# Attention and greedy expert routing on one core: the first matrix product of the last two experts as seven block products

## The chip, the core and the metric

The kernel runs on one core of a Trainium2 chip. The metric is the device time of one execution in microseconds (us). The core has five engines with a queue each: PE (matrix multiply; its weight loads are shown as PEld), DVE (vector), ACT (activation), POOL (GpSimd) and SP, which here only starts DMA transfers and reads registers. An engine works through its queue in order; engines wait for each other through semaphores.

## The reference, cut to what matters

Clustered attention gives `x` (3072 tokens of 512). Each of 8 experts takes 384 tokens, chosen greedily by gate logits, and puts them through two matrix products with a ReLU between them:

```python
for e in range(E):                       # E = 8, cap = 3072 // 8 = 384 tokens each
    mask = assigned == e
    h = np.maximum(x[mask] @ w1[e], 0.0) # (384 x 512) @ (512 x 1024)
    out[mask] = h @ w2[e]                # (384 x 1024) @ (1024 x 512)
```

Inputs, weights and outputs are float32.

## The kernel before

The attention is the first part of the program and is not touched. In the second part the experts follow each other; in step names `p` is the place in this sequence (0 to 7), so "the last two experts" are p = 6 and p = 7. Which expert stands at a place, and which tokens it takes, is worked out on DVE with small PE products (steps `b`, `ind`, `cnt`, `c1` to `c3`, `gt`, `ge`, `rank`, `scan`, `col`, `pb0`, `pb1`, `rep`, `idx` and others), while the expert before is computed.

**Float32 as two float16.** Every operand is split into a high part, its value rounded to float16, and a low part, the rest. A product is three PE products: high by high, high by low, low by high.

**Work of one expert p.**
- `reg` reads the number of the expert into a register of SP; `w_load,p,c` loads eight 512 KB chunks of float32 weights into `wr0` to `wr7` (chunks 0 to 3: w1, 128 of the 512 input rows each; chunks 4 to 7: w2).
- `wsc` scales a chunk in place on ACT, `whi` writes its high part on ACT (`w1h`, `w2h`), `wlo` subtracts on POOL and writes its low part (`w1l`, `w2l`). These have two buffers each, by p % 2.
- `gx,p,g` fetches 128 tokens (indirect DMA, started by POOL), `xt` transposes them into `xgt` (started by SP). `xgt` holds high and low parts, 384 token columns each.
- `hid,p,f,c,i`: one PE product of 128x128 weights with 384 columns; f is one of 8 blocks of 128 hidden units, c one of 4 input chunks, i one of the three split products. 96 of these make the hidden layer of an expert. Their result lies in PSUM (`pf`, a pool of 5 banks).
- `rel,p,f` (ACT) writes the high part of ReLU, `hh`; `hlo,p,f` (DVE) the low part, `hl`.
- `out,p,g,f,i`: one PE product for 128 tokens g and hidden block f with 512 columns; 24 for each g, 72 for an expert. For p = 7, g = 2 it is cut in 384 and 128 columns (a fifth argument, 0 or 1).
- `oev` (ACT) scales the result into `ot`, `sc` (POOL) starts the indirect DMA that scatters it to the output.

**Order.** `FFN_ORDER` is one text of steps, executed one after the other when the program is built. Each step appends its instructions to its engine's queue, so the text fixes the order on every engine; the steps of different engines only wait for data and buffers. Before the change the text runs `hid` and `out` of p = 5, 6, 7 one after the other, with `rel`, `hlo`, `oev`, weight preparation and routing strewn in.

The routing state lies in PSUM (`pk`, one bank), so most DVE instructions of routing have a PSUM operand; `hlo` reads PSUM as well.

## Time and profile before

| what | value |
|---|---|
| time, median of 3 runs | 678.59 us (677.88 to 680.59) |
| time of the profiled execution | 678.19 us |
| span of its instructions | 676.4 us |
| mean granted TensorE clock | 0.969 |
| PE, DVE, ACT, POOL busy | 637.9, 498.5, 421.3, 512.9 us |

The span goes from the first to the last instruction; what lies between it and the execution's own time is 1.8 us. "Busy" adds up the recorded durations without their overlaps. A PE matmul is recorded from its issue to its modelled end, and the next is issued long before that, so the distance between two starts tells what a matmul costs, not its duration. A granted clock of 1 is 2.4 GHz, one of 0.5 is 1.2 GHz.

### The profile page before, as it was taken

Reading aid. Unit: us, or ns where it says so; the run is one execution under the profiler, and the core shown is the slowest. Engines: PE = TensorE matmul, PEld = TensorE weight load, DVE = VectorE, ACT = ScalarE, POOL = GpSimd, SP = SyncE. Lnnn points to the kernel's source line nnn. Section 1 sums busy time; section 2 is a strip of 40 time slices with the busy share of each in tenths; the row PEclk is TensorE's granted clock in tenths of the full one; section 3 lists DMA queues with packets and bytes.
Section 4 is the critical chain, followed back from the end, with each engine's and each line's share of the span. In section 5 each row is a group of like instructions: output and inputs, shape, how many; then the busy total and the mean of one; then the engine's idle time right before and its main releaser. Section 6 shows DMA issues by size and latency. Waiting matters only on the chain. (4 is left out here: it accounts for less than half of the span.)

```text
span 676.4 us, 19511 instructions
## 1 busy us (share of the span) xinstructions
PE 637.9 (94%) x8154; PEld 428.9 (63%) x8154; DVE 498.5 (74%) x1096; ACT 421.3 (62%) x560; POOL 512.9 (76%) x452
## 2 busy tenths in 40 slices
...
GB/s 239 140 144 199 210 156 214 144 149 206 207 115 177 196 143 100 167 73 74 29 51 72 25 234 108 267 105 286 182 209 226 179 222 168 240 302 206 47 1 47
DMA packets 175451, 105.85 MB, mean 156 GB/s; under 512 B 135426, under 2 KB 160002, under 8 KB 175362
## 3 DMA queue, kind: packets, MB, share of 16 engines
...
q8 instruction: 64, 1.05, 0.7%
q14 instruction: 25, 0.20, 0.1%
...
## 5 line engine op out<-in xcount | busy, mean ns | idle before, releaser
L842 POOL TENSOR_TENSOR rt<-pt 128x768 f16<-128x768 f32 x180 | 276.5, 1558 | 26.6 <-ACT pt L834 25.8
L834 ACT ACTIVATE pt<-sc 128x768 f32<-128x768 f32 x192 | 149.8, 811 | 93.9 <-PE sc L831 73.5
L792 DVE TENSOR_REDUCE mxs<-sc 128x1 f32<-128x768 f32 x192 | 176.1, 951 | 17.7 <-PE sc L788 17.2
L1457 PE MATMUL pf<-xgt,w1h 128*128 128x384 f16 (+1 forms) x640 | 130.2, 295 | 0.3 <-DVE xgt L752 0.2
L856 PE MATMUL av<-vh,rt 128*128 128x65 f16 x1152 | 120.6, 193 | 1.7 <-POOL rt L842 1.6
L853 PE MATMUL av<-vh,pt 128*128 128x65 f16 x1152 | 120.7, 194 | 1.1 <-DVE xb L889 1.1
L855 PE MATMUL av<-vl,pt 128*128 128x64 f16 x1152 | 120.4, 191 | 0.0
L855 PEld LDWEIGHTS <-pt 128*128 128x128 bf16 x1152 | 105.8, 98 | 8.6 <-issue 1.5
L853 PEld LDWEIGHTS <-pt 128*128 128x128 bf16 x1152 | 106.2, 97 | 7.3
L856 PEld LDWEIGHTS <-rt 128*128 128x128 f16 x1152 | 105.3, 97 | 1.9 <-POOL rt L842 1.9
L827 PE MATMUL sc<-qbt,kbt 99*128 99x384 f16 x384 | 94.4, 327 | 1.3 <-DVE mxs L792 0.7
L831 PE MATMUL sc<-qat,kat 128*128 128x384 f16 x384 | 94.4, 327 | 0.0
L788 PE MATMUL sc<-kbt,qbt 80*128 80x384 f16 x384 | 90.5, 330 | 2.2 <-DVE qbt L752 0.5
L1457 PE MATMUL pf<-xgt,w1l 128*128 128x384 f16 (+1 forms) x320 | 89.9, 295 | 0.0
L1415 ACT ACTIVATE wr<-wr 128x1024 f32<-128x1024 f32 x64 | 66.7, 1046 | 25.9 <-DMA wr<-in_moe_w_dram 25.3
L1457 PEld LDWEIGHTS <-w1h 128*128 128x128 f16 x640 | 58.0, 98 | 28.3 <-issue 0.9
L1499 PE MATMUL pf<-w2h,hh 128*128 128x512 f16 (+2 forms) x200 | 73.6, 370 | 0.0
L1499 PE MATMUL pf<-w2l,hh 128*128 128x512 f16 (+2 forms) x200 | 73.6, 370 | 0.0
L1499 PE MATMUL pf<-w2h,hl 128*128 128x512 f16 (+2 forms) x200 | 73.2, 370 | 0.0
L1425 POOL TENSOR_TENSOR w2l<-wr,w2h 128x1024 f16<-128x1024 f32 x32 | 67.6, 2133 | 7.3 <-ACT w2h L1418 6.8
L1425 POOL TENSOR_TENSOR w1l<-wr,w1h 128x1024 f16<-128x1024 f32 x32 | 67.4, 2133 | 1.5 <-ACT w1h L1418 1.3
L1489 DVE SCALAR_TENSOR_TENSOR hl<-pf,hh 128x384 f16<-128x384 f32 x56 | 30.9, 553 | 45.7 <-ACT hh L1486 40.2
...
## 6 DMA issues: line engine op xcount, KB each, us to landing
...
xg<-xrow,idx POOLq DMA_INDIRECT x24, 6.5
```

The source lines that it names most:

```text
L788: nc.tensor.matmul(p[:, half, :S // 2], QBT[u][:D + C, i, :], KBT[u][:D + C, h * J + half * 3:h * J + half * 3 + 3, :], start=True, stop=True)
L792: nc.vector.tensor_reduce(mxs[u % 3][:, i:i + 1], MP.pop((u, i))[:, :, :S // 2], axis=AX.XY, op=OP.max)
L827: nc.tensor.matmul(ps[:, half, :S // 2], KBT[u][:ER + 3, s, :], QBT[u][:ER + 3, cs, :], start=True, stop=False)
L831: nc.tensor.matmul(ps[:, half, :S // 2], KAT[u][:, s, :], QAT[u][:, cs, :], start=False, stop=True)
L834: nc.scalar.activation(pts[(u * 12 + s // 2) % RP][:, s % 2], MP.pop((u, "b", s))[:, :, :S // 2], AF.Exp, scale=ESC)
L842: (nc.vector if e == "D" else nc.gpsimd).tensor_sub(rts[x][:, s % 2], p.rearrange("p a b -> p (a b)"), hi_view(pts[x])[:, s % 2])
L853: nc.tensor.matmul(o[:, j, :D + 1], hi[:, js], VH[u][:, s, :D + 1], start=(kt == 0 and j == 0), stop=False, skip_group_check=True)
L855: nc.tensor.matmul(o[:, j, :D], hi[:, js], VL[u][:, s, :], start=False, stop=False, skip_group_check=True)
L856: nc.tensor.matmul(o[:, j, :D + 1], r[:, js], VH[u][:, s, :D + 1], start=False, stop=(kt == J - 1), skip_group_check=True)
L1425: nc.gpsimd.tensor_sub(lo, wrs[c], hi)
L1457: nc.tensor.matmul(o, (w1l if i == 2 else w1h)[x][:, c, fs], xgt[x][:, h + int(i == 1), ts], start=(first and i == 0), stop=(last and i == ...
L1499: nc.tensor.matmul(PS["o", p, g], (hl if i == 2 else hh)[x][:, f, g * P:(g + 1) * P], (w2l if i == 1 else w2h)[x][:, f, ds], start=(f == 0 ...
```

## The change

For p = 6 and p = 7 the 96 `hid` products, the `rel` and `hlo` steps, and `whi` and `wlo` of chunks 0 to 3 are gone. The product of w1 (transposed, 1024 x 512) with the tokens (512 x 384) is cut in 2 x 2 blocks: hidden halves by input halves for the weights (A11, A12, A21, A22), input halves by halves of 192 tokens. Seven block products replace eight, after the scheme of Strassen in Winograd's form:

- `sS,p,n,k` (DVE): the weight sums S1 = A22 + A21, S3 = A11 - A21, S2 = S1 - A11, S4 = A12 - S2, in float32, in place in `wr0` to `wr3`; k is one of two chunks, 512 columns each.
- `sh` (ACT) and `sl` (DVE or POOL, by its last letter D or P): high and low part of a block, 512 columns; A11, A12, A22 and the four sums, two chunks each, 14 of each step for an expert. The high parts lie in `sxh` or `w1h`, the low ones in `sxl` or `w1l`.
- `tx` (DVE): tokens high + low, float32, 1536 columns, into the `hh` buffer; `tt,p,n` (DVE): the token differences T1 to T4 (384 columns) into the `hl` buffer; `th` (ACT) and `tl` (DVE): their high and low part into `tsp`.
- `sp,p,n,q` (PE): block product n for half q of its hidden blocks: 12 matmuls of 192 columns; 14 such steps for an expert. M1, M6, M5, M3 add up in one bank `Z` for each q, M2 goes to `Y`, M7 and M4 to `X`.
- `cy` (ACT) copies `Z` between these additions to `zc`; `ad` (DVE) adds such a copy to `Y` or `X` into `sm`; `re` (ACT) and `hs` (DVE) write the high and low part of ReLU into `hh` and `hl`, eight of each (384 columns).

All steps of the text from `hid,5,2,0,1` on stand in another order: `hid,5` and `out,5` are mixed, the routing of p = 7 stands earlier or later, `out,6` and `out,7` run over all three g at once, `sc,5,1`, `sc,5,2` and `sc,6,2` stand much later. The steps themselves of p = 5, of the second products and of the routing are the same. In `f_out` and `f_oev` the key of the PSUM tile gets the part w of the columns, since both parts of p = 7, g = 2 are now open at the same time.

```diff
...
-oev,7,2,1 sc,7,2
...
+out,7,1,2,0 out,7,0,0,0 out,7,0,0,1 out,7,0,0,2 out,7,2,0,0,0 out,7,0,1,0 out,7,2,0,1,0 out,7,2,0,2,0 out,7,2,1,0,0
...
+    SH = F // 2
+    sxh, sxl = (ex.tile([P, 3, 2, SH], F16, name=n) for n in ("sxh", "sxl"))
+    tsp = ex.tile([P, 4, 2, 2, CAP // 2], F16, name="tsp")
+    zcs = [ex.tile([P, 2, CAP // 2], F32, name=f"zc{i}") for i in range(4)]
+    sms = [ex.tile([P, 2, CAP // 2], F32, name=f"sm{i}") for i in range(2)]
+    HOME = {"A11": 0, "A12": 1, "S2": 2, "S1": 0, "S3": 1, "S4": 2, "A22": 3}
+    RAW = {"A11": (0, 0), "A12": (0, 2), "A22": (1, 2), "S1": (1, 2), "S2": (0, 0), "S3": (1, 0), "S4": (0, 2)}
+    SUMS = {1: ((1, 2), (1, 0), (1, 2), OP.add), 3: ((1, 0), (0, 0), (1, 0), OP.subtract),
+            2: ((0, 0), (1, 2), (0, 0), OP.subtract), 4: ((0, 2), (0, 2), (0, 0), OP.subtract)}
+    half = (slice(0, CAP // 2), slice(CAP // 2, CAP))
+
+    def sraw(r, k):
+        return wrs[r[1] + k][:, r[0] * SH:(r[0] + 1) * SH]
+
+    def shome(p, b, k):
+        h = HOME[b]
+        if b in ("A11", "A12", "S2"):
+            return sxh[:, h, k, :], sxl[:, h, k, :]
+        c, o = 2 * (h // 2) + k, (h % 2) * SH
+        return w1h[p % 2][:, c, o:o + SH], w1l[p % 2][:, c, o:o + SH]
+
+    def f_sh(p, b, k):
+        nc.scalar.activation(shome(p, b, k)[0], sraw(RAW[b], k), AF.Copy)
+
+    def f_sl(p, b, k, e):
+        hi, lo = shome(p, b, k)
+        (V if e == "D" else nc.gpsimd).tensor_sub(lo, sraw(RAW[b], k), hi)
+
+    def f_sS(p, n, k):
+        o, a, b, op = SUMS[n]
+        V.tensor_tensor(sraw(o, k), sraw(a, k), sraw(b, k), op=op)
+
+    def sxf(p):
+        return hh[p % 2].rearrange("p f n -> p (f n)").bitcast(F32).rearrange("p (c n) -> p c n", c=DC)
+
+    def stt(p, n):
+        t = hl[p % 2].rearrange("p f n -> p (f n)").bitcast(F32).rearrange("p (t c n) -> p t c n", t=4, c=2)
+        return t[:, n - 1]
+
+    def f_tx(p):
+        x = xgt[p % 2].rearrange("p (c w) n -> p c w n", w=2)
+        V.tensor_tensor(sxf(p), x[:, :, 0, :], x[:, :, 1, :], op=OP.add)
+
+    def f_tt(p, n):
+        x = sxf(p)
+        b = lambda j, l: x[:, 2 * j:2 * j + 2, half[l]]
+        l, r = {1: (b(0, 1), b(0, 0)), 2: (b(1, 1), stt(p, 1)), 3: (b(1, 1), b(0, 1)), 4: (b(1, 0), stt(p, 2))}[n]
+        V.tensor_tensor(stt(p, n), l, r, op=OP.subtract)
+
+    def f_th(p, n):
+        nc.scalar.activation(tsp[:, n - 1, :, 0, :], stt(p, n), AF.Copy)
+
+    def f_tl(p, n):
+        V.tensor_tensor(tsp[:, n - 1, :, 1, :], stt(p, n), tsp[:, n - 1, :, 0, :], op=OP.subtract)
+
+    PROD = {1: ("A11", (0, 0)), 2: ("A12", (1, 0)), 3: ("S4", (1, 1)), 4: ("A22", 4), 5: ("S1", 1), 6: ("S2", 2), 7: ("S3", 3)}
+    ACC = {1: "Z", 6: "Z", 5: "Z", 3: "Z", 2: "Y", 7: "X", 4: "X"}
+
+    def f_sp(p, n, q):
+        blk, t = PROD[n]
+        z, first, last = ACC[n], n in (1, 2, 7), n in (3, 2, 4)
+        if first:
+            PS[z, q] = pff.tile([P, 2, CAP // 2], F32, name="pf")
+        for m in range(2):
+            fs = slice((2 * q + m) * P, (2 * q + m + 1) * P)
+            for k in range(2):
+                h, l = shome(p, blk, k)
+                if isinstance(t, int):
+                    xh, xl = tsp[:, t - 1, k, 0, :], tsp[:, t - 1, k, 1, :]
+                else:
+                    xh, xl = (xgt[p % 2][:, 2 * (2 * t[0] + k) + w, half[t[1]]] for w in range(2))
+                for i, (a, b) in enumerate(((h, xh), (h, xl), (l, xh))):
+                    nc.tensor.matmul(PS[z, q][:, m, :], a[:, fs], b, start=(first and m == 0 and k == 0 and i == 0),
+                                     stop=(last and m == 1 and k == 1 and i == 2), skip_group_check=True)
+
+    def f_cy(p, i, q, s):
+        nc.scalar.activation(zcs[s], PS["Z", q], AF.Copy)
+
+    def f_ad(p, z, q, s, o):
+        V.tensor_tensor(sms[o], PS[z, q], zcs[s], op=OP.add)
+
+    def sout(t, p, b, q):
+        i, l = b // 2, b % 2
+        f = 4 * i + 2 * q
+        return t[p % 2][:, f:f + 2, half[l]]
+
+    def f_re(p, b, q, o):
+        nc.scalar.activation(sout(hh, p, b, q), PS["Z", q] if o is None else sms[o], AF.Relu)
+
+    def f_hs(p, b, q, o):
+        V.scalar_tensor_tensor(sout(hl, p, b, q), PS["Z", q] if o is None else sms[o], 0.0, sout(hh, p, b, q),
+                               op0=OP.max, op1=OP.subtract)
+
...
     def f_out(p, g, f, i, w=2):
         ds = span(w)
         if f == 0 and i == 0:
-            PS["o", p, g] = pff.tile([P, ds.stop - ds.start], F32, name="pf")
+            PS["o", p, g, w] = pff.tile([P, ds.stop - ds.start], F32, name="pf")
         x = p % 2
-        nc.tensor.matmul(PS["o", p, g], (hl if i == 2 else hh)[x][:, f, g * P:(g + 1) * P], (w2l if i == 1 else w2h)[x][:, f, ds],
+        nc.tensor.matmul(PS["o", p, g, w], (hl if i == 2 else hh)[x][:, f, g * P:(g + 1) * P], (w2l if i == 1 else w2h)[x][:, f, ds],
                          start=(f == 0 and i == 0), stop=(f == FC - 1 and i == 2))
 
     def f_oev(p, g, w=2):
-        nc.scalar.activation(ots[(3 * p + g) % 4][:, span(w)], PS["o", p, g], AF.Copy, scale=1.0 / (SX * SW * SW))
+        nc.scalar.activation(ots[(3 * p + g) % 4][:, span(w)], PS["o", p, g, w], AF.Copy, scale=1.0 / (SX * SW * SW))
```

**PE, first product of p = 6.** What stood on PE before, in `hid` of p = 6 (`w1h_8026` and `w1l_8028` are the buffers of p = 6, `pf` the PSUM bank, `xgt_8038` the tokens):

```order
L1457 LDWEIGHTS w1h_8026
L1457 MATMUL pf<-xgt_8038,w1h_8026 128x384
L1457 LDWEIGHTS w1l_8028
L1457 MATMUL pf<-xgt_8038,w1l_8028 128x384
L1457 LDWEIGHTS w1h_8026
L1457 MATMUL pf<-xgt_8038,w1h_8026 128x384
```

and what stands there now, in `sp,6,2,1` (`sxh`, `sxl` hold the parts of A12):

```order
L1543 LDWEIGHTS sxh
L1543 MATMUL pf<-xgt_8038,sxh 128x192
L1543 LDWEIGHTS sxh
L1543 MATMUL pf<-xgt_8038,sxh 128x192
L1543 LDWEIGHTS sxl
L1543 MATMUL pf<-xgt_8038,sxl 128x192
```

Each matmul has half the columns, and there are 168 where 96 were; every one has its own weight load, as before.

**DVE, behind the routing of p = 7.** Before, from `ohv,7` (L1342) on; L1369 to L1382 are `pb0`, `pb1`, `pi`, `idx`, L1489 is `hlo`:

```order
L1342 TENSOR_TENSOR ohv<-ohl,pk 128x384
L1369 TENSOR_TENSOR cq_8009<-pc,own_189 128x192
L1372 TENSOR_REDUCE cs_8010<-cq_8009 128x24
L1379 SCALAR_TENSOR_TENSOR pg<-pc,own_189 128x24
L1382 TENSOR_REDUCE idx_8017<-pg 128x3
L1489 SCALAR_TENSOR_TENSOR hl_8042<-pf,hh_8040 128x384 x8
L1489 SCALAR_TENSOR_TENSOR hl_8043<-pf,hh_8041 128x384 x8
```

Now, behind `pb1,7`, during the block products of p = 6 (L1512 `tx`, L1518 `tt`, L1497 `sl`, L1501 `sS`, L1524 `tl`, L1370 and L1373 `pi`, `idx`, L1550 `ad`; `hh_8040` and `hl_8042` hold sums of tokens here, `tsp` the parts of T1 to T4):

```order
L1512 TENSOR_TENSOR hh_8040<-xgt_8038 128x1536
L1518 TENSOR_TENSOR hl_8042<-hh_8040 128x384 x2
L1497 TENSOR_TENSOR sxl<-wr_8018,sxh 128x512
L1518 TENSOR_TENSOR hl_8042<-hh_8040,hl_8042 128x384
L1501 TENSOR_TENSOR wr_8021<-wr_8021,wr_8019 128x512
L1524 TENSOR_TENSOR tsp<-hl_8042,tsp 128x2x192 x2
L1370 SCALAR_TENSOR_TENSOR pg<-pc,own_189 128x24
L1373 TENSOR_REDUCE idx_8017<-pg 128x3
L1550 TENSOR_TENSOR sm_8057<-pf,zc_8053 128x384
L1550 TENSOR_TENSOR sm_8058<-pf,zc_8054 128x384
L1524 TENSOR_TENSOR tsp<-hl_8042,tsp 128x2x192
L1497 TENSOR_TENSOR w1l_8028<-wr_8020,w1h_8026 128x512
```

Where two `idx` instructions and then the `hlo` of the expert stood, there are now 14 instructions: `tx` stands behind `pb1,7`, and everything that T1 to T4 need stands behind `tx` in the same queue; most of these instructions read two operands that both lie in SBUF.

**POOL, the last rows.** Before (L1425 `wlo`, L1506 `sc`; `w2l1` the low parts of w2 of p = 7, `ot2`, `ot3` and so on the results that are scattered):

```order
L1425 TENSOR_TENSOR w1l1_8029<-wr3_8021,w1h1_8027 128x1024
L1425 TENSOR_TENSOR w2l1_8033<-wr4_8022,w2h1_8031 128x1024
L1425 TENSOR_TENSOR w2l1_8033<-wr5_8023,w2h1_8031 128x1024
L1425 TENSOR_TENSOR w2l1_8033<-wr6_8024,w2h1_8031 128x1024
L1506 DMA out_0_dram<-ot2_8048,idx2_8016 3072x512
L1425 TENSOR_TENSOR w2l1_8033<-wr7_8025,w2h1_8031 128x1024
L1506 DMA out_0_dram<-ot3_8049,idx2_8016 3072x512
L1506 DMA out_0_dram<-ot0_8046,idx2_8016 3072x512
```

and now (L1497 `sl`, L1416 `wlo`, L1590 `sc`; `w1l1` the low parts of sums of p = 7):

```order
L1497 TENSOR_TENSOR w1l1_8029<-wr1_8019,w1h1_8027 128x512
L1497 TENSOR_TENSOR w1l1_8029<-wr3_8021,w1h1_8027 128x512 x2
L1416 TENSOR_TENSOR w2l1_8033<-wr4_8022,w2h1_8031 128x1024
L1590 DMA out_0_dram<-ot3_8049,idx2_8016 3072x512
L1416 TENSOR_TENSOR w2l1_8033<-wr5_8023,w2h1_8031 128x1024
L1416 TENSOR_TENSOR w2l1_8033<-wr6_8024,w2h1_8031 128x1024
L1416 TENSOR_TENSOR w2l1_8033<-wr7_8025,w2h1_8031 128x1024
L1590 DMA out_0_dram<-ot0_8046,idx2_8016 3072x512
L1590 DMA out_0_dram<-ot1_8047,idx3_8017 3072x512
L1590 DMA out_0_dram<-ot2_8048,idx3_8017 3072x512
```

The scatter `sc,6,1` (from `ot3`) stands between the first and the second w2 subtraction of p = 7, and the other three stand behind it.

## Rows read from the trace of the kernel before

**Rows 1.** The page's first part: busy time, share of the span, instructions.

```profile
PE 637.9 (94%) x8154; PEld 428.9 (63%) x8154; DVE 498.5 (74%) x1096; ACT 421.3 (62%) x560; POOL 512.9 (76%) x452
```

**Rows 2.** Windows from `hid,5,2` on: length, busy (instructions) by engine, clock, DMA, GB/s.

```profile
579.40:600.00 20.60, 20.60 (x122) 11.12 (x120) 15.31 (x51) 15.59 (x21) 11.77 (x8) 1.00 0.94 289
600.00:620.00 20.00, 20.00 (x116) 11.08 (x115) 4.00 (x9) 17.72 (x23) 16.57 (x12) 1.00 0.93 295
620.00:640.00 20.00, 20.00 (x102) 9.67 (x101) 1.67 (x3) 7.87 (x11) 16.25 (x10) 1.00 0.15 53
640.00:660.00 20.00, 20.00 (x116) 11.25 (x115) 4.46 (x8) 4.25 (x9) 0.74 (x1) 1.00 0.04 14
```

**Rows 3.** PE timeline: start, duration, line, form, count; widths 384, 128, 192.

```profile
611.78 0.33 PE L1457 MATMUL pf<-xgt,w1l 128*128 128x384 f16 x1
...
622.99 0.33 PE L1457 MATMUL pf<-xgt,w1l 128*128 128x384 f16 x1
...
668.55 0.22 PE L1499 MATMUL pf<-w2h,hh 128*128 128x128 f16 x1
...
669.84 0.22 PE L1499 MATMUL pf<-w2h,hl 128*128 128x128 f16 x1
...
585.05 0.42 PE L1365 MATMUL pc<-ohh,ohv 128*128 128x192 f16 x3
585.31 0.33 PE L1457 MATMUL pf<-xgt,w1h 128*128 128x384 f16 x1
```

**Rows 4.** The page's groups: weight loads of the first product.

```profile
L1457 PEld LDWEIGHTS <-w1h 128*128 128x128 f16 x640 | 58.0, 98 | 28.3 <-issue 0.9
```

**Rows 5.** Groups by form: line, operation, form, count | busy us, mean ns.

```profile
L877 DVE TENSOR_TENSOR av<-av,rc 128x384 f32<-128x384 f32 x31 | 17.6, 566 | 1.0
L1478 DVE SCALAR_TENSOR_TENSOR hl<-pf,hh 128x512 f16<-128x512 f32 x6 | 4.1, 685 | 0.1
L657 DVE SCALAR_TENSOR_TENSOR qa<-ld,qa 128x1536 f16<-128x1536 f32 x6 | 10.5, 1755 | 0.6 <-ACT qa L652 0.5
L1415 ACT ACTIVATE wr<-wr 128x1024 f32<-128x1024 f32 x64 | 66.7, 1046 | 25.9 <-DMA wr<-in_moe_w_dram 25.3 <-issue 0.6
L652 ACT ACTIVATE qa<-ld 128x384 f16<-128x384 f32 x4 | 2.1, 523 | 0.1
L1425 POOL TENSOR_TENSOR w2l<-wr,w2h 128x1024 f16<-128x1024 f32 x32 | 67.6, 2133 | 7.3 <-ACT w2h L1418 6.8
L659 POOL TENSOR_TENSOR qa<-ld,qa 128x384 f16<-128x384 f32 x4 | 3.6, 912 | 0.5 <-ACT qa L652 0.4
```

**Rows 6.** Timelines of POOL and DVE, attention: subtractions with both operands in SBUF.

```profile
339.84 2.89 POOL L842 TENSOR_TENSOR rt<-pt 128x768 f16<-128x768 f32 x2
...
343.06 5.74 POOL L842 TENSOR_TENSOR rt<-pt 128x768 f16<-128x768 f32 x3
...
343.39 4.09 DVE L842 TENSOR_TENSOR rt<-pt 128x768 f16<-128x768 f32 x2 [1.07 <-ACT pt L834]
...
359.86 3.68 DVE L842 TENSOR_TENSOR rt<-pt 128x768 f16<-128x768 f32 x4
```

**Rows 7.** PE and DVE timelines around the routing of p = 6.

```profile
586.12 0.33 PE L1457 MATMUL pf<-xgt,w1h 128*128 128x384 f16 x1
586.44 0.17 PE L1376 MATMUL pc<-cs,rep 128*128 128x24 f16 x1
...
579.53 0.40 DVE L1290 SCALAR_TENSOR_TENSOR mk<-pk,pc,mq 128x24 bf16<-128x24 f32 x2
...
585.91 0.48 DVE L1372 TENSOR_REDUCE cs<-cq 128x24 f16<-128x192 f16 x1
```

**Rows 8.** Timelines of POOL and SP: token fetches and transposes of p = 6.

```profile
587.43 0.98 POOL L1429 DMA_INDIRECT xg<-xrow,idx  x1 [9.29 <-DVE idx L1382]
...
594.98 5.36 SPq L1433 DMA_TRANSPOSE xgt<-xg  x3
```

**Rows 9.** Window at the switch from attention to experts, columns as in Rows 2.

```profile
375.00:380.00 5.00, 1.25 (x36) 1.11 (x32) 4.13 (x21) 0.00 (x0) 0.00 (x0) 0.56 0.15 43
```

More of the change, by code (lines that the diff above doesn't have):

```diff
@@ L368 @@
-hid,5,3,3,2 hid,5,4,0,0 ohl,6 w_load,6,5 hid,5,4,0,1 rel,5,3 hid,5,4,0,2 hid,5,4,1,0 ohh,6 hid,5,4,1,1 w_load,6,6
-hid,5,4,1,2 hid,5,4,2,0 hid,5,4,2,1 ohv,6 w_load,6,7 hid,5,4,2,2 hid,5,4,3,0 lt,6 col,6 wsc,6,0 upd,6 hid,5,4,3,1
-hid,5,4,3,2 pb0,6 hid,5,5,0,0 hid,5,5,0,1 hid,5,5,0,2 pb1,6 hid,5,5,1,0 rel,5,4 hlo,5,3 rep,6 hid,5,5,1,1 hid,5,5,1,2
-whi,6,0,C hid,5,5,2,0 pi,6 hid,5,5,2,1 hid,5,5,2,2 idx,6 hid,5,5,3,0 hlo,5,4 gx,6,0 hid,5,5,3,1 hid,5,5,3,2
-hid,5,6,0,0 wsc,6,1 b,7,0 hid,5,6,0,1 hid,5,6,0,2 hid,5,6,1,0 b,7,1 hid,5,6,1,1 hid,5,6,1,2 gx,6,1 b,7,2 hid,5,6,2,0
```

122 lines of the change are left out of this document (59 added, 63 removed).

## The prediction, on record before the changed kernel was run

> **What bounds the kernel now.** I read the page's first part first: PE is busy for 94% of the span, the next engines for 76% and 74% [rows 1]. That is a mean over unlike stages, so next came windows over the changed part, from `hid,5,2,0,1` at 579.4 us (call it T) on. There PE is busy all of the time at a granted clock of 1.00, while DVE has 15.3, 4.0, 1.7 and 4.5 us of work in stretches of 20, and POOL's load ends by 640 [rows 2]. The reader is to see that only PE sets the time here, and that the others have room, DVE most. Then I measured starts on the PE timeline, because a duration of a matmul overlaps the next: 69 matmuls of 384 columns take 622.99 - 611.78 = 11.21 us, 0.1625 each; 23 of 128 columns take 1.29, 0.0561 each [rows 3]. A line through both is 0.416 ns a column, which gives 0.0827 for 192 and 0.216 for 512. The only 192-column products are three of `col`; with the step to the next instruction they take 0.26, 0.087 each at most [rows 3]. Last I looked at waits: at `rep,6` PE stands 0.16 us beyond a matmul's 0.1625, behind the reduction `pb1,6` on DVE [rows 7]. From T the matmuls need about 90.5 us, to 669.84 + 0.22 = 670.06 [rows 3]. Behind them comes the last result and scatter, which the change leaves alone.
>
> **What it takes away and adds on PE.** An expert loses 96 x 0.1625 = 15.6 us and gets 14 x 12 = 168 matmuls of 192 columns, 168 x 0.0827 = 13.9. That is 1.7 less, for two experts **-3.4 us**. With 0.087 it is 168 x 0.087 = 14.6, together -2.0; with columns alone (7/8 of 15.6) it is -3.9. I take -3.4, since 384 and 128 columns lie on one line and 192 lies between. Weight loads number 168 where 96 stood. One is recorded with 98 ns [rows 4], yet matmuls of 128 columns, each with its own load, go by every 56 ns, so loads are hidden at a shorter distance than 83 ns.
>
> On that the Trainium skill disagrees ("TensorE: Matmul & The Clock Gate", section "Back-to-back issue gap"): it gives about 81 ns for each matmul of 128 columns and 131 for 512 in a stream with a load for each. On a straight line between them, an estimate, 192 columns would cost 89 ns and 384 some 114, and the two experts would lose 8 us. The trace has 56 and 162 ns for 128 and 384 columns, so I go by the rows.
>
> **What it adds elsewhere, hidden or not.** For both experts together DVE gets about 60 instructions more. By the nearest rows (0.57 for 384 columns, 0.69 for 512, 1.76 for 1536 [rows 5]) its work from T rises from 27 to 66 us, ACT's (0.52 for 384, some 0.63 for 512, 1.05 for 1024 [rows 5]) from 50 to 70; POOL keeps 48 (2.13 for 1024, 0.91 for 384, so 1.1 to 1.2 for 512 [rows 5]). All are below the 86.6 us that PE has to do from T on (90.0 before by counts, less 3.4), so the sums cost nothing; if anything costs, it is the order at single places. I put PE's steps in their new order with the prices above and walked the other queues against them; times are us behind T.
>
> 1. `rep,6`. PE gets there at 6.9. `pb1,6` ended at 7.0 before (585.91 + 0.48 less T) [rows 7]; now `hlo,5,1` and more routing stand ahead, I reckon 7.3. PE waits 0.5 where it waited 0.2: **+0.3**. If the walk is off, 0 to 1.
>
> 2. Block products of p = 6. `col,7` is on PE at 23.9 (71 `hid`, 53 `out`, 1 `sp` to `sp,6,2,1` and the routing's few). `pb1` ends 1.4 behind it, as it did for p = 6 (585.05 to 586.39 [rows 3, 7]), so at 25.3. Behind it on DVE stand `tx` 1.76, three `tt` 1.7, `sl` 0.69, `sS` 0.69, two `tl` 1.13, `pi` and `idx` 0.35 (an estimate from 0.20 for 24 columns [rows 7]), two `ad` 1.13, `tl` 0.57 and `sl,6,S1,0` 0.69: 8.7, ending at 34.0. PE needs the last of them for `sp,6,5,1`, at 34.7 by content (71 `hid`, 72 `out`, 7 `sp`), 35.2 with the wait above. So there is 1.2 us of room. Two things use it up. `tx` also needs the third token transpose: `gx,6,2` starts at about 13.8 on POOL, fetch to transpose takes 7.6 and a transpose occupies the queue for 1.8, three take 5.36 [rows 8], and SP issues weight loads beside it; it lands between 24 and 26, which is **+0.3** at most likely, 0 to 0.8. And `tx`, `tt`, `tl`, `sl`, `sS` read two SBUF operands, as POOL's subtractions do. Two such on DVE and POOL took turns in the attention: POOL alone took 1.45 each, overlapped 1.91; DVE alone 0.92, overlapped 2.04, so 1.1 more for each that meets one [rows 6]. POOL has `sl,6,S1,1` and `sl,6,S3,1` in this stretch, and perhaps `wlo,6,4`; two meetings are 2.2, beyond the room by 1.0. I take half of it, **+0.5**, with 0 and 5 as bounds (5: all of POOL's 2.13 + 2 x 1.2, and the fetches late too).
>
> The Trainium skill has this as a rule ("SBUF — State Buffer", section "Who interferes with whom"): a DVE instruction with two SBUF inputs and a GpSimd one share an exclusive lock, and the second waits in full. The trace agrees, with 0.92 against 2.04. By the rule in full it is the rival B below.
>
> 3. w2 of p = 7. POOL has `wlo,7,4`, `sc,6,1`, `wlo,7,5` to `wlo,7,7` at its end. `sc,6,1` waits for `oev,6,1`, which ACT ends at about 71.3, behind `whi,7,6`. A scatter's issue taken like a fetch's 0.98 [rows 8] and two `wlo` of 2.13 [rows 5] end at 76.6; with one meeting with DVE's `hs` on the way `wlo,7,6` is done at 77.0. A chunk of w2 serves two hidden blocks, so chunk 6 is first read by `out,7,0,4,1`: at 76.4 by content, a few tenths later with the waits so far. I take **+0.4**, 0 to 1.5. `wlo,7,7` at 79.2 to 79.7 then stands against `out,7,0,6,1` at 79.9.
>
> 4. Banks, given back by ACT and DVE between block products, and `tl,7,4`: **+0.2**, 0 to 1. Elsewhere the walk leaves 1 to 3 us.
>
> Together +1.7. The change is -3.4 + 1.7 = -1.7: the profiled 678.19 becomes 676.5. The median of the runs stands 0.4 above the profiled time, so I say **676.9 us**. For the clock I count nothing: it stood at 0.56 where PE was busy for 1.25 of 5 us [rows 9], and waits of tenths between full stretches are far from that.
>
> **Rivals.**
> - A, everything is on time: no wait beyond before's 0.2. 678.6 - 3.4 = 675.2. For it: sums of work on DVE and ACT are far below PE's. Against it: at places 1 and 3 the queues arrive at the same time as PE.
> - C, the gain is used up: places 2 and 3 near their upper bounds by turns, waits of 2.5 to 5.5 in all, 677.7 to 680.7. For it: two chains with 1 us of room each, worked out by hand.
> - B, slower: in the block products of p = 6 DVE loses its turns to POOL. Ten two-operand instructions stand between `pb1,7` and `sp,6,5,1`; if seven meet a POOL subtraction, 7 x 1.1 = 7.7, less the room of 1.2, is 6.5, and the same in the products of p = 7, where DVE is loaded as much, some 2 more, with 0.9 from places 1 and 3: waits of 8 to 9.5 and 678.6 - 3.4 + 8 = 683 or more. It decides when all waits exceed 3.4, and makes it slower by more than 0.5% from 6.8 on. Against it: POOL has only two to four subtractions in those 9 us, so at most four can meet.
> - D, weight loads bind: 168 x 0.098 = 16.5 against 15.6, +0.9 for each expert, 678.6 + 1.7 + 1.7 = 682.0. Against it stand the 56 ns of 128 columns [rows 3, 4].
>
> **How the numbers follow.** The forecast (675.5 to 678) has 0.60, A 0.16, C 0.13, B 0.09, D 0.02. The range of 675.0 to 680.0 holds the forecast, A's upper part and most of C, and leaves out B, D and the ends. Half a per cent, about what a measurement here can tell from no change, is 3.4 us: faster than 675.2 needs all of A and a bit of the pure column price, 0.11; slower than 682.0 is B and half of D, 0.09; the rest is 0.80. So it most likely gains a quarter of a per cent.
>
> **What would show it.** Starts of the 192-column products lie 0.083 apart (0.098 would be D). Gaps on PE stand at `rep,6`, ahead of S1 T1 in p = 6 (behind DVE), and at `out,7,0,4,1` (behind POOL), each under 1 us, and the granted clock stays at 1.00 to the end. POOL's `sl` and `wlo` and DVE's `tx`, `tl`, `sS` would last longer where they overlap; if DVE's are over 1.5 us in a row, it is B. If `tx,6` waits for a transpose and not for `pb1`, place 2 fails in its cause. A matmul end that moved by less than the sum of waits would make the columns' price wrong.

## The result, and the profile after

The changed kernel takes 688.27 us (median of 5 runs, 686.46 to 691.56) where the kernel before took 678.87 in the same comparison: a ratio of 1.0149, 95% interval 1.0118 to 1.0181. It is 9.4 us slower; 676.9 had been forecast. The profiled execution took 691.56 us, the longest of the five, with a span of 689.8 against 676.4. Of these 13.4 us, 2.8 stand ahead of everything that the change touches: the matmuls of the two traces drift apart at 15 to 25 us, in the attention, and the distance is still 2.77 where `hid,5,2,0,1` starts, at 582.17 (T) here and at 579.40 before. What follows counts from T. From T to the end of the span the changed kernel takes 107.6 us, the kernel before 97.0.

The page's first part after the change; it answers to [rows 1]:

```profile
PE 641.3 (93%) x8298; PEld 442.1 (64%) x8298; DVE 550.3 (80%) x1156; ACT 436.3 (63%) x600; POOL 516.3 (75%) x458
```

DVE has 51.8 us more than before. Waiting inside two of its instructions accounts for 10.3 of them, as will be seen. Windows of the changed kernel from T on, with the columns of [rows 2]:

```profile
582.17:622.40 40.23, 39.92 (x303) 26.54 (x300) 33.39 (x79) 31.27 (x51) 26.27 (x20) 1.00 0.70 229
622.40:627.00 4.60, 0.37 (x5) 0.14 (x3) 4.50 (x4) 0.16 (x1) 3.99 (x3) 0.86 0.94 246
627.00:632.50 5.50, 5.50 (x29) 4.22 (x28) 3.43 (x7) 5.47 (x10) 0.99 (x1) 0.50 1.12 268
632.50:666.70 34.20, 33.76 (x263) 22.91 (x262) 32.58 (x42) 23.25 (x41) 13.71 (x9) 1.00 0.09 33
666.70:670.00 3.30, 1.08 (x5) 0.31 (x4) 3.30 (x2) 0.00 (x0) 3.13 (x3) 1.00 0.00 0
670.00:673.50 3.50, 3.50 (x11) 1.34 (x10) 0.09 (x1) 0.00 (x0) 0.48 (x1) 0.52 0.20 75
673.50:681.80 8.30, 8.28 (x59) 4.68 (x56) 0.00 (x0) 1.57 (x3) 1.94 (x2) 1.00 0.09 34
681.80:689.80 8.00, 0.00 (x0) 0.00 (x0) 0.00 (x0) 0.30 (x2) 0.97 (x1) 0.62 0.17 66
```

The reader is to see two holes and what lies behind each. From 622.40 PE does almost nothing for 4.6 us while DVE and POOL are busy; then its granted clock is 0.50 for 5.5 us. From 666.70 the same again, shorter, with 0.52 for 3.5 us behind it. PE's rows at both holes and at `rep,6` (the last number in brackets is the idle time and who ended it):

```profile
589.02 0.33 PE L1448 MATMUL pf<-xgt,w1h 128*128 128x384 f16 x1
589.65 0.17 PE L1367 MATMUL pc<-cs,rep 128*128 128x24 f16 x1 [0.31 <-DVE cs L1363]
...
622.39 0.25 PE L1543 MATMUL pf<-xgt,w1l 128*128 128x192 f16 x1
626.86 0.50 PE L1543 MATMUL pf<-tsp,w1h 128*128 128x192 f16 x2 [4.23 <-DVE sm L1550]
...
667.17 0.38 PE L1583 MATMUL pf<-w2l,hh 128*128 128x512 f16 x1
669.67 0.39 PE L1583 MATMUL pf<-w2h,hl 128*128 128x512 f16 x1 [2.12 <-DVE hl L1561]
```

Start to start, less the product's own 0.08 or 0.216, the holes are 4.40 us (`sp,6,4`, A22 by T4) and 2.29 us (`out,7,0,4,2`, the first that reads `hs,7,2,0`). What DVE and POOL did there:

```profile
620.64 5.04 DVE L1524 TENSOR_TENSOR tsp<-hl,tsp 128x384 f16<-128x384 f32 x1 [0.24 <-ACT tsp L1521]
...
663.27 6.82 DVE L1561 SCALAR_TENSOR_TENSOR hl<-sm,hh 128x384 f16<-128x384 f32 x2
```

```profile
620.06 0.96 POOL L1420 DMA_INDIRECT xg<-xrow,idx  x1 [0.16 <-issue]
621.05 4.21 POOL L1416 TENSOR_TENSOR w2l<-wr,w2h 128x1024 f16<-128x1024 f32 x2
...
661.64 1.24 POOL L1590 DMA_INDIRECT out_dram<-ot,idx  x1 [3.34 <-ACT ot L1587]
662.91 6.28 POOL L1416 TENSOR_TENSOR w2l<-wr,w2h 128x1024 f16<-128x1024 f32 x3
```

`tl,6,4` takes 0.55 us elsewhere and 5.04 here: it ends 0.4 us behind the second of two w2 subtractions on POOL (621.05 + 4.21 = 625.26). The `hs` of p = 7, 0.55 elsewhere, stands at 663.27 and ends 0.4 us behind the third of three (669.19). `ad,6,X,0,0,0`, which the first hole names as releaser, is only the next but one behind `tl,6,4` in DVE's queue.

The sum, from T to the last matmul 99.61 us (to 681.78), where 90.66 had been needed, so 8.95 more (the first three terms give 9.0):

| term | us |
|---|---|
| 336 products of 192 columns at 0.0825 for 192 of 384 at 0.1625 | -3.5 |
| waits of PE: `rep,6` 0.47; `sp,6,4` 4.40; `sp,7,4` 0.39 + 0.38; `out,7,0,4,1` 0.26; `out,7,0,4,2` 2.29; less 0.22 before (0.16 of it at `rep,6`) | +8.0 |
| half clock behind the two long waits: 2.8 and 1.7, added up start to start against the prices at 1.00 | +4.5 |
| last matmul to the end of the span: 8.00 for 6.36 | +1.6 |
| together | +10.6 |

The last term was no part of the forecast either. POOL's scatters and ACT's results at the end of the changed kernel:

```profile
676.22 0.97 POOL L1590 DMA_INDIRECT out_dram<-ot,idx  x1 [5.74 <-ACT ot L1587]
680.53 0.97 POOL L1590 DMA_INDIRECT out_dram<-ot,idx  x1 [3.34 <-issue]
684.01 0.97 POOL L1590 DMA_INDIRECT out_dram<-ot,idx  x1 [2.51 <-issue]
```

```profile
675.35 0.60 ACT L1587 ACTIVATE ot<-pf 128x512 f32<-128x512 f32 x1 [11.70 <-PE pf L1583]
677.72 0.60 ACT L1587 ACTIVATE ot<-pf 128x512 f32<-128x512 f32 x1 [1.78 <-PE pf L1583]
681.42 0.68 ACT L1587 ACTIVATE ot<-pf 128x384 f32<-128x384 f32 x2 [3.10 <-PE pf L1583]
```

The first result is ready at 675.95 and its scatter starts 0.27 us later. The other two are ready at 678.3 and 682.1, yet their scatters start at 680.53 and 684.01, about 2 us later. In the kernel before the last scatter started 0.27 us after its result (670.38 and 670.65).

### The profile page after: what moved, and what is told of

Its sections match the earlier page's. It is cut to its first block, busy times and chain, and to the rows that moved or that the text cites. A ratio compares the mean times of both kernels' runs of the same rounds, so it can differ in the third digit from the quotient of the medians.

```text
span 689.8 us, 19884 instructions
## 1 busy us (share of the span) xinstructions
PE 641.3 (93%) x8298; PEld 442.1 (64%) x8298; DVE 550.3 (80%) x1156; ACT 436.3 (63%) x600; POOL 516.3 (75%) x458
## 5 line engine op out<-in xcount | busy, mean ns | idle before, releaser
L1448 PE MATMUL pf<-xgt,w1h 128*128 128x384 f16 (+1 forms) x512 | 99.5, 288 | 0.3 <-DVE xgt L743 0.2
L1416 POOL TENSOR_TENSOR w2l<-wr,w2h 128x1024 f16<-128x1024 f32 x32 | 67.9, 2145 | 8.5 <-ACT w2h L1409 8.1
L1448 PE MATMUL pf<-xgt,w1l 128*128 128x384 f16 (+1 forms) x256 | 69.3, 288 | 0.0
L1583 PEld LDWEIGHTS <-hh 128*128 128x128 f16 x400 | 37.8, 99 | 34.9 <-issue 2.4
L1448 PEld LDWEIGHTS <-w1h 128*128 128x128 f16 x512 | 45.7, 99 | 20.1 <-issue 0.7
L1590 POOL DMA_INDIRECT out_dram<-ot,idx x24 | 24.7, 1030 | 42.7 <-ACT ot L1587 33.6
```

Of the source, the lines that this page charges most:

```text
L1416: nc.gpsimd.tensor_sub(lo, wrs[c], hi)
L1448: nc.tensor.matmul(o, (w1l if i == 2 else w1h)[x][:, c, fs], xgt[x][:, h + int(i == 1), ts], start=(first and i == 0), stop=(last and i == ...
L1583: nc.tensor.matmul(PS["o", p, g, w], (hl if i == 2 else hh)[x][:, f, g * P:(g + 1) * P], (w2l if i == 1 else w2h)[x][:, f, ds], start=(f = ...
```

## The experiments

Each kernel was timed beside the kernel before. The last column is the time from T to the end of the span in the profiled execution (97.0 in the kernel before). T itself lies between 577.97 (a1) and 582.97 (c3) in these profiles, though the attention is the same in all, so the medians of a few executions carry scatter that the last column leaves out; it comes from one execution each. Where the intervals of two ratios overlap, as those of a1, a2 and a3 do with the changed kernel's, the times alone don't tell them apart, and the argument rests on the traces.

| kernel | median us | before us | ratio (95%) | T to end, us |
|---|---|---|---|---|
| changed kernel | 688.27 | 678.87 | 1.0149 (1.0118 to 1.0181) | 107.6 |
| a1_whi_late | 684.79 | 677.68 | 1.0119 (1.0100 to 1.0138) | 102.7 |
| a2_w2l_dve | 684.54 | 677.68 | 1.0110 (1.0090 to 1.0130) | 103.4 |
| a3_fill | 684.35 | 677.68 | 1.0118 (1.0087 to 1.0150) | 104.2 |
| a4_wlo_first | 687.26 | 677.68 | 1.0156 (1.0139 to 1.0173) | 104.2 |
| c1_dve_all | 684.68 | 679.32 | 1.0082 (1.0057 to 1.0106) | 102.2 |
| c2_dve_tail | 682.65 | 679.32 | 1.0060 (1.0026 to 1.0094) | 101.2 |
| c3_whi76_late | 691.02 | 679.32 | 1.0171 (1.0144 to 1.0197) | 109.6 |
| c4_order | 686.80 | 679.32 | 1.0106 (1.0068 to 1.0144) | 105.9 |
| d1_late_tail | 681.11 | 678.37 | 1.0036 (1.0015 to 1.0057) | 99.4 |
| d2_whi76 | 686.72 | 678.37 | 1.0126 (1.0088 to 1.0164) | 104.8 |
| d3_no_pool | 680.97 | 678.37 | 1.0040 (1.0025 to 1.0055) | 99.3 |
| d4_no_sl | 677.99 | 678.37 | 0.9995 (0.9978 to 1.0012) | 97.1 |
| e1_oev_early | 680.99 | 679.39 | 1.0024 (1.0011 to 1.0036) | 97.8 |
| e3_hs_early | 680.95 | 678.52 | 1.0034 (1.0015 to 1.0052) | 97.8 |

**The wait at `sp,6,4`.** In a1_whi_late POOL's first w2 subtraction is held back until `tl,6,4` can have its turn:

```diff
 re,6,0,1,1 cy,6,b,0,2
-whi,6,7,C
 wlo,6,5,C
...
 th,6,4
+whi,6,7,C
 tl,6,4
```

> One step is moved on ACT: whi,6,7 stands behind th,6,4, so POOL's wlo,6,7 cannot start before th,6,4 is done, and DVE's tl,6,4 (5.04 us in the changed kernel, beside two wlo of POOL from 621.05 to 625.25) gets its turn ahead of them. Theory 1 (POOL's run of subtractions keeps DVE's two-SBUF instruction out, and the clock falls to 0.50 because PE stood still): tl,6,4 takes under 1 us, PE's wait of 4.40 us ahead of sp,6,4 shrinks under 1 us, and the stretch at half clock behind it (2.9 us lost) is gone too; with the p = 7 part as it was, the median goes from 688.3 to about 681 (680 to 683). Theory 2 (tl,6,4 is late because T4 itself or its high part comes late): the wait stays above 3 us and the time within 1 us of 688.3. Theory 3 (the clock falls for a reason of its own): the wait goes, the half clock stays, about 684.

DVE's rows of a1_whi_late, and POOL's:

```profile
616.39 0.56 DVE L1524 TENSOR_TENSOR tsp<-hl,tsp 128x384 f16<-128x384 f32 x1 [0.84 <-ACT tsp L1521]
617.75 2.23 DVE L1561 SCALAR_TENSOR_TENSOR hl<-sm,hh 128x384 f16<-128x384 f32 x1 [0.80 <-ACT hh L1558]
620.09 0.56 DVE L1550 TENSOR_TENSOR sm<-pf,zc 128x384 f32<-128x384 f32 x1
```

```profile
617.44 4.53 POOL L1416 TENSOR_TENSOR w2l<-wr,w2h 128x1024 f16<-128x1024 f32 x2 [0.65 <-issue]
```

`tl,6,4` takes 0.56 us, so theory 2 is out: T4 was not late by itself. But PE's wait shrank only to 2.48, because the next DVE instruction, `hs,6,0,0,0`, now met POOL (2.23 us for 0.55), and behind it stands `ad,6,X,0,0,0`, which must read the bank X before `sp,6,4` may add to it. No stretch at half clock came in the profiled execution, which was the fastest of the four (682.54). Against the kernel before, the median is 7.1 us slower where the changed kernel was 9.4: 2.3 us were gained, where 7 had been expected.

a4_wlo_first and c4_order ask how the two engines take turns. In a4 the run of two starts ahead of the fetch and `tl,6,4` asks inside it; in c4 the second of the run is besides released only after `tl,6,4` has asked:

```diff
+wlo,6,7,C wlo,6,6,C
 gx,7,2
...
-wlo,6,7,C
...
-wlo,6,6,C
```

> POOL's wlo,6,7 and wlo,6,6 stand ahead of the token fetch gx,7,2 and not behind it; so the run of two begins about 1 us earlier, right behind a subtraction and not behind a fetch, and DVE's tl,6,4 becomes ready inside the first of them. Theory 1a (POOL keeps its turn through a whole run): tl,6,4 waits for the end of both, some 3.5 us, PE waits about 3.3 instead of 4.4: time 686.5 to 688. Theory 1b (turns alternate between instructions, as at 343 us in the attention and at 653 in the changed kernel, unless DVE's instruction came before the run): tl,6,4 waits for the first only, about 1.4 us, PE waits 1 to 1.5 and the clock may hold: 681.5 to 685.

> As the run in which wlo,6,7 and wlo,6,6 stand ahead of gx,7,2, where tl,6,4 came 0.78 us into the first of them and had to wait for both (3.85 us); now whi,6,6 on ACT stands behind th,6,4 as well, so wlo,6,6 is released only after tl,6,4 has asked, but before wlo,6,7 ends. Theory 'in the order of release' (an instruction stands behind all those of the other engine that were released before it, and ahead of those released later): tl,6,4 runs after wlo,6,7, in 1.2 to 2 us, and wlo,6,6 comes behind it, stretched. Theory 'POOL goes on as long as it has a ready instruction': tl,6,4 still waits for both, 3.3 us or more. For the time: PE's wait ahead of sp,6,4 falls from 3.2 to 1 to 2 us in the first case, 685 to 687, and stays in the second.

The second edit, of c4 alone:

```diff
-whi,6,6,C
...
 th,6,4
+whi,6,6,C
 tl,6,4
```

In a4 `tl,6,4` came 0.78 us into the first and took 3.85 us, PE waited 3.21: theory 1a for this run of two. DVE, POOL and ACT in c4:

```profile
617.99 3.86 DVE L1524 TENSOR_TENSOR tsp<-hl,tsp 128x384 f16<-128x384 f32 x1 [0.23 <-ACT tsp L1521]
```

```profile
617.20 4.22 POOL L1416 TENSOR_TENSOR w2l<-wr,w2h 128x1024 f16<-128x1024 f32 x2
```

```profile
617.85 1.05 ACT L1409 ACTIVATE w2h<-wr 128x1024 f16<-128x1024 f32 x1
```

`whi,6,6` ended at 618.90, so `wlo,6,6` was free only 0.9 us after DVE had asked (617.99), and DVE still stood behind it until 621.42. "In the order of release" is refuted; here POOL went on as long as it had a ready instruction (the `hs` of a1, which was let in behind the first of two, is taken up at the end).

**The wait in `out,7`.** a2_w2l_dve moves three subtractions from POOL to DVE, at the same places:

```diff
-            nc.gpsimd.tensor_sub(lo, wrs[c], hi)
+            (V if v == "D" else nc.gpsimd).tensor_sub(lo, wrs[c], hi)
...
-wlo,7,5,C
+wlo,7,5,D
```

(and so for 6 and 7).

> The three last low parts of w2 of p = 7 (wlo,7,5 to wlo,7,7) are computed on DVE in place of POOL, at the same places of the text; POOL has no subtraction left while hs,7,2,0 and hs,7,2,1 are due. Theory 1 (lock): hs,7,2,0 takes 0.55 and not over 6 us, PE's wait of 2.29 us in out,7 and the half clock behind it (2.0 us) go, waits for the three DVE subtractions (some 1.2 us each) of 0 to 0.8 us take their place: about 684 (683 to 686) against 688.3. Theory 2 (hs is late because of its inputs): the wait of over 2 us stays, and DVE's longer queue adds to it: 688 or more.

The two `hs` took 0.55 each, and behind `sp,7,4` PE had no wait at all up to the last product; the wait at `sp,6,4` stayed at 4.41.

```profile
661.99 1.02 DVE L1561 SCALAR_TENSOR_TENSOR hl<-sm,hh 128x384 f16<-128x384 f32 x2
```

The time, 684.54, is what the lock theory gave. d2_whi76 reaches the same instruction without moving work:

```diff
-whi,7,6,C
...
 re,7,2,0,0
+whi,7,6,C
 hs,7,2,0,0 out,7,0,4,0
```

> One step moved on ACT in the changed kernel: whi,7,6 stands right behind re,7,2,0 (in the run whi76_late it stood one product too late in the text, so that out,7,0,4,0 read an older high part of w2 and held the step back). wlo,7,6 is then not ready while hs,7,2,0 asks. Lock theory: hs,7,2,0 waits for wlo,7,5 at most, under 2 us in place of 6.35; PE's wait ahead of out,7,0,4,2 goes from 2.3 us to under 0.5, with 0.3 to 0.8 us for wlo,7,6; 1 to 4 us less than the changed kernel (more where the half clock came behind that wait). Rival: hs,7,2,0 stays above 5 us.

```profile
658.74 2.80 DVE L1561 SCALAR_TENSOR_TENSOR hl<-sm,hh 128x384 f16<-128x384 f32 x1
```

The first `hs` took 2.80 us, behind a scatter and one subtraction in place of 6.35 behind three (under 2 had been expected); the wait ahead of `out,7,0,4,2` is gone, and the granted clock stays at 1.00 there. But `wlo,7,6` now ran only from 663.78 to 665.90, and PE waited 1.60 for it, not 0.3 to 0.8: most of the wait came back in another place. Its forerunner c3_whi76_late had the step one product later, so that `out,7,0,4,0` used an older high part of w2 and `whi,7,6` had to wait for it. Its `hs` took 2.80 us as well, but PE then waited 3.51 us for `wlo,7,6`, so its time says nothing of the gain.

**The clock by itself.** a3_fill gives PE products without use in both holes and leaves the late DVE instructions as they are:

```diff
+dm,64
 sp,6,4,0
...
+dm,32
 out,7,0,4,2
...
+    def f_dm(n):
+        d = pct.tile([P, P], F32, name="pc")
+        for _ in range(n):
+            nc.tensor.matmul(d, ident, ident, start=True, stop=True)
```

> PE gets work without use in its two long waits: 64 products of 128 columns (3.6 us) ahead of sp,6,4 and 32 (1.8 us) ahead of out,7,0,4,2, into a free PSUM bank; all else as in the changed kernel. If the granted clock falls because PE stands still, both half-clock stretches (2.9 and 2.0 us lost) vanish while DVE's late instructions stay as late: 683.5 (682.5 to 685). If the clock falls for another reason, the stretches stay and the time is 688.3 or a little more. If the filling lengthens the waits, 689 or more.

Windows of a3_fill over both holes and what follows them:

```profile
618.00:622.50 4.50, 4.50 (x77) 4.50 (x76) 4.50 (x2) 0.89 (x2) 4.33 (x3) 1.00 1.01 270
622.50:628.00 5.50, 4.14 (x38) 2.86 (x35) 4.78 (x10) 4.59 (x8) 0.60 (x1) 1.00 1.10 169
661.00:664.50 3.50, 3.31 (x39) 2.26 (x37) 3.50 (x1) 0.00 (x0) 3.33 (x3) 1.00 0.00 0
664.50:668.00 3.50, 3.24 (x16) 1.58 (x17) 0.67 (x2) 0.00 (x0) 1.06 (x1) 1.00 0.20 75
```

`tl,6,4` and `hs` were as late as before (5.06 and 6.36 us), and the granted clock is 1.00 throughout. In the six other profiles with a wait of 3.2 to 4.4 us at `sp,6,4` (the changed kernel, a2, a4, c3, c4, d2) a stretch below 1.00 stands behind it (0.50 to 0.72 on average over the next 3 to 6 us). So the half clock came from PE standing still. From T to the end a3 takes 104.2 us where the changed kernel takes 107.6: 3.4 us came back. The median is 684.35, at the upper part of what was expected.

**Five subtractions off POOL, and the tail.** c1_dve_all is a2 with `wlo,6,6` and `wlo,6,7` on DVE as well; c2_dve_tail besides moves eight products of `out,7` (from `out,7,1,2,1` to `out,7,1,4,0`) behind `out,7,0,7,2`:

```diff
-out,7,1,2,1 out,7,1,2,2
 out,7,0,5,0
...
-out,7,2,1,1,0 out,7,2,1,2,0 out,7,1,3,0 out,7,1,3,1 out,7,1,3,2 out,7,1,4,0
...
 out,7,0,7,2
+out,7,1,2,1 out,7,1,2,2 out,7,2,1,1,0 out,7,2,1,2,0 out,7,1,3,0 out,7,1,3,1 out,7,1,3,2 out,7,1,4,0
```

> The five subtractions of w2 that kept DVE out (wlo,6,6, wlo,6,7 and wlo,7,5 to wlo,7,7) are computed on DVE in place of POOL, at the same places of the text. Lock theory: neither tl,6,4 nor hs,7,2,0 lasts over 1.5 us; PE's waits of 4.4 and 2.3 us and the half clock go; what is left are the waits of some tenths (0.5 at rep,6, about 1.7 in the block products of p = 7) and the tail of 7.7 to 8.0 us in place of 6.36. That gives the time of before, minus 3.4, plus 2.2 plus 1.5, so 0.3 us above the kernel before, -1 to +2. A rival: DVE, with 6 us more work, becomes late itself, and the time stays 4 us or more above the kernel before.

> As the run before (five subtractions on DVE), and eight products of out,7 (six of 512 columns, two of 384) move behind out,7,0,7,2, so that the result of g = 0 is complete 1.6 us earlier. Theory of the tail: each scatter waits for the landing of the one before (3.5 to 4.1 us from issue to the next issue), so three results that are complete within 6.5 us queue up; with g = 0 earlier, the last scatter starts 0.3 us after its result, as before the change, and the time from the last matmul to the end falls from 7.7 or 8.0 to 6.4 to 6.7 us: 1.3 us less than the run before. Rival (the delay of 1.9 us is of the last scatter itself, its issue or its data): the tail stays at 7.7 to 8.0.

In c1 no DVE instruction waited for those subtractions and the half clock was gone, but it is 5.4 us above the kernel before, not 0.3: waits of 1.83 us in `out,6` and of 2.09 and 1.08 in the first block products of p = 7 came up. The first is for `hs,6,1,1`, which stands in DVE's queue behind one of the moved subtractions and an `sl`, the second for a bank that ACT's `oev,6,0` gives back behind three `th`, which wait for DVE. So far the rival was right. The third is POOL again: `sl,7,S2,0` on DVE asked during a scatter of POOL and ended 0.56 us behind the two `sl` of POOL that followed it, 3.32 us for 0.69.

```profile
645.04 3.32 DVE L1497 TENSOR_TENSOR sxl<-wr,sxh 128x512 f16<-128x512 f32 x1
```

In c2 the tail is 6.37 us (7.91 in c1), as the theory of the tail gave. Its last three scatters:

```profile
667.32 0.97 POOL L1590 DMA_INDIRECT out_dram<-ot,idx  x1 [4.31 <-ACT ot L1587]
671.31 0.97 POOL L1590 DMA_INDIRECT out_dram<-ot,idx  x1 [3.02 <-ACT ot L1587]
675.09 0.97 POOL L1590 DMA_INDIRECT out_dram<-ot,idx  x1 [2.81 <-ACT ot L1587]
```

All are now released by ACT's result, 0.27 us before, while the row of `sc,6,2`, whose result was ready earlier, names the landing of the scatter before it:

```profile
661.84 1.17 POOL L1590 DMA_INDIRECT out_dram<-ot,idx  x1 [2.00 <-DMA out_dram<-ot,idx]
```

**What is left.** d1_late_tail joins the edits of a1, a2 and c2's tail. d3_no_pool is c2 with the four `sl` of p = 7 and `wlo,7,4` on DVE too, and `hs,6,1,1` right behind `re,6,1,1`. d4_no_sl is d3 without the 14 `sl` of p = 7 (it leaves these low parts out). e1_oev_early is d3 with `oev,6,0` right behind `out,6,0,7,2` and `wlo,6,6` ahead of `wlo,6,7`; e3_hs_early is e1 with `re,6,2` and `hs,6,2` ahead of both. One line of each edit, d3 against c2, e1 against d3 and e3 against e1:

```diff
-sl,7,S2,1,P
+sl,7,S2,1,D
```

```diff
+wlo,6,6,D
 wlo,6,7,D
...
 out,6,0,7,2
+oev,6,0
 sh,7,S3,1
```

```diff
+re,6,2,0,0 re,6,2,1,1 hs,6,2,0,0 hs,6,2,1,1
 wlo,6,6,D wlo,6,7,D
```

> Three edits that were run singly, together: whi,6,7 behind th,6,4; wlo,7,5 to wlo,7,7 on DVE; the eight products of out,7 behind out,7,0,7,2. If the waits are independent, PE's waits from the routing of p = 6 on are 0.5 + 2.5 + 0.7 + 0.9 + 0.9, about 5.4 us, the tail is 6.4 us and there is no half clock: 0.5 to 2.5 us above the kernel before. Rival: with less waiting in p = 6, DVE is late in the block products of p = 7 by as much more (as with all five subtractions on DVE, where 2.1 and 1.1 us came up there), and the time stays 4 us above.

> As dve_tail, and POOL has no subtraction left behind the block products of p = 6: the four sl of p = 7 that were POOL's and wlo,7,4 are on DVE too, and hs,6,1,1 stands ahead of two sl and three sums on DVE, right behind re,6,1,1. DVE does 512 columns in 0.69 us where it waited 1.0 to 2.6 us for POOL. Theory (DVE and POOL together are one resource in this stage, and the cheaper engine should do the work): the wait of 1.8 us in out,6 goes, those ahead of the block products of p = 7 (2.1, 1.1, 0.9 us) fall to 2 us together: 0 to 2 us above the kernel before. Rival (DVE is full as it is, more work makes it later): 3 us above or more.

> As no_pool, but the 14 sl of p = 7 are left out: the low parts of its weight blocks are not computed and the products take what lies in the buffers, so DVE has 9.6 us less to do there, while PE does the same products. Theory (DVE's work sets the pace of p = 7): PE's waits ahead of and in the block products of p = 7 go below 0.5 us, and the time is 3.4 less 1 to 1.5, so 1.5 to 2.5 us BELOW the kernel before: what the seven products are worth on PE when the other engines keep up. Rival (PE waits for ACT, loads or banks): the waits there stay and the time stays above the kernel before.

> As no_pool, with two more steps in another place: oev,6,0 on ACT stands right behind the last product of out,6,0 and no longer behind sh,7,S3,1 and three th, and wlo,6,6 stands ahead of wlo,6,7 on DVE, because out,6,2,4,1 reads chunk 6 first. If the wait of 2.05 us ahead of sp,7,2 was for the bank that oev,6,0 gives back, and that of 1.65 us in out,6 for wlo,6,6, both go: 3 to 3.5 us less than no_pool, which lies 2.6 above the kernel before, so 0 to 1.2 us BELOW the kernel before. Rival (each removed wait is replaced by the next late step on DVE, as in the runs so far): 1 to 2 us less than no_pool, still above the kernel before.

> As oev_early, and re,6,2 and hs,6,2 (both halves) stand ahead of the two w2 subtractions of p = 6 on their engines, because the wait of 1.9 us in out,6 that was left there was for hs,6,2,0,0, behind tx,7 and others in DVE's queue. If the rest are single hand-offs, this wait goes and 1.2 to 1.9 us with it: 0 to 0.6 us below the kernel before, and PE's waits from the routing of p = 6 on sum to 2.5 us or less. Rival (DVE, with hardly an idle moment between 624 and 644 us, is full: what PE no longer waits for in out,6 it waits for ahead of the block products of p = 7): the time stays within 0.6 us of oev_early, 1 to 2 us above the kernel before.

d1 has the tail of 6.37 and PE waits of 4.5 us, but its profiled execution still lost 1.7 us to half clock around the 2.48 us at `sp,6,4`; at 1.0036 it is near the edge of what was expected. d3 came out at 1.0040, between the two theories; `hs,6,1,1` was no longer waited for, a w2 low part was (1.65 us), and 2.05 us ahead of `sp,7,2` were for a bank that ACT's `oev,6,0` gives back. e1 took out both and got 1.5 us from T on, since 1.90 for `hs,6,2,0,0` and 1.12 for a bank from `oev,6,2` came in their place; e3 took out the first of these and got nothing. PE's rows of e1 and then of e3 show the wait wander:

```profile
634.71 0.39 PE L1583 MATMUL pf<-w2h,hl 128*128 128x512 f16 x1 [1.74 <-DVE hl L1561]
```

```profile
640.11 0.25 PE L1543 MATMUL pf<-xgt,sxl 128*128 128x192 f16 x1
641.85 0.33 PE L1543 MATMUL pf<-xgt,sxh 128*128 128x192 f16 x2 [1.49 <-ACT ot L1587]
```

The sum of PE's waits from the routing of p = 6 on was 4.5 us in e1 and 4.4 in e3. A window of e1 over the second product of p = 6 and the beginning of p = 7:

```profile
623.90:643.60 19.70, 17.01 (x109) 9.67 (x107) 18.60 (x28) 15.73 (x26) 2.60 (x2) 1.00 0.50 125
```

The same for d3 and then d4, up to the wait ahead of `sp,7,2`:

```profile
623.90:640.80 16.90, 15.13 (x85) 7.68 (x84) 14.29 (x21) 12.24 (x20) 1.51 (x1) 1.00 0.48 142
623.90:638.70 14.80, 14.55 (x84) 7.48 (x82) 11.60 (x17) 12.06 (x19) 1.28 (x1) 1.00 0.51 149
```

DVE is busy for 18.6 of 19.7 us in e1, more than PE with 17.0. With the `sl`, in d3, it is busy for 14.3 of 16.9 us; without them, in d4, for 11.6 of 14.8 with the same products, the wait for a w2 low part is gone, and from T on the time falls by 2.2 us, to no difference from the kernel before (0.9995). 1.7 us ahead of `sp,7,2` remained there, for `oev,6,0` behind ACT's other steps, so the 1.5 to 2.5 us below the kernel before were not reached; d4 with e1's earlier `oev,6,0` was not run. No version that computes everything was faster than the kernel before; the best, e1, is 0.24% slower (e3, whose interval overlaps, 0.34%).

## Why the prediction was wrong

**PE's own price: right.** The 192-column products of the changed kernel start 7.84 us apart over 95 intervals (651.12 to 658.96), 0.0825 each; 0.0827 was taken, and -3.4 measured -3.5. Weight loads did not bind at 82.5 ns, so rival D (98) is out. The 89 ns that the prediction estimated by a straight line through the figures of the Trainium skill ("TensorE: Matmul & The Clock Gate", section "Back-to-back issue gap") are not what this stream took.

**The places that were costed: three of four nearly right.** `rep,6` waited 0.47 (0.5 forecast), `out,7,0,4,1` 0.26 (0.4). S1 by T1 in p = 6, where 0.8 was put, had no wait at all: `tx`, the sums and the `sl` came through just in time, POOL met `tx` for 0.3 us only. Place 4, banks and `tl,7,4`, had been given 0.2: `sp,7,4` waited 0.77 within its bounds of 0 to 1, but `sp,6,4`, also a bank that DVE gives back, 4.40.

**"So 1.1 more for each that meets one": the step that failed.** It came from [rows 6], where DVE and POOL took turns one by one, and it put the bound of a meeting at one subtraction. Where POOL had several ready, DVE could wait for the whole run: 4.5 us beyond its own time for `tl,6,4`, 5.8 for the `hs` of p = 7. Both places had been passed over with "0.2, 0 to 1" and "elsewhere the walk leaves 1 to 3 us", margins that would have covered one meeting and didn't cover a run of two or three. a1, a2 and d2 show it from both sides: with the run broken or taken away, the instruction takes 0.55 to 2.8 us. Rival B had the cause (DVE losing its turns to POOL) and the sign, with 0.09, but at 1.1 us a meeting it asked for seven; two sufficed.

**"For the clock I count nothing": wrong.** The fall had been seen in [rows 9], and a wait of 4.4 us was not in the forecast. Once it came, the clock cost 4.5 us on top of 6.7; a3, with the holes filled, keeps 1.00.

**"Which the change leaves alone": wrong.** The tail's steps are the same, but the order that finishes three results within 6.2 us puts their scatters in a queue: 1.6 us, and c2 takes them out, against c1, by products moved alone.

**"So the sums cost nothing": too kind.** DVE's 66 us came out (77.3 from T on, 10.3 of them the waiting inside `tl,6,4` and `hs`), but 66 of 86.6 is a mean over the stretch. In the changed kernel PE has no wait from the end of the first hole to `sp,7,4`, so this is no part of the 9.4 us; it is what keeps the repairs from winning. Between the block products of p = 6 and p = 7 DVE has as much work as PE once the subtractions are moved off POOL; c1, e1 and e3 show that a removed wait comes back elsewhere, on DVE or on ACT behind it, and d4 that DVE's relief lets a part of it go. In the forecast the sum of queues had been compared with PE from T to the end, and the walk costed four places, not this stage. Whether an order exists that keeps the 3.4 us is not settled: the best order tried still leaves 4.4 us of waits, and many others are possible.
